# Linear attention with a token and channel mixer: kv products of two late units in one string, and weights split straight from their fp64 bits

## The chip, the cores and the metric

The kernel runs on one core of one Trainium2 chip. The metric is device time in microseconds (us) of one execution. Three runs of the kernel before gave 778.94, 780.80 and 781.54 us; their median is 780.8 us. Engines go by the profile's names: PE is TensorE (matrix products), PEld its weight loads, DVE is VectorE, ACT is ScalarE, POOL is GpSimd, and SP is SyncE, whose only work here is to issue DMAs in order.

## The reference

```
q, k, v: (8 batches, 8 heads, 576 rows, 64), float32
qs = softmax of q over the 64 columns;   ks = softmax of k over the 576 rows
kv = ks^T v     (64 x 64 for each head); attn = qs kv
x  = attn as (8, 576, 512)
h  = relu(x^T w_tok1) w_tok2;            u   = x + h^T     (w_tok1 576 x 256)
h2 = relu(u w_ch1) w_ch2;                out = u + h2      (w_ch1 512 x 1536)
```

The four weight matrices arrive as 64-bit floats and are brought to 32 bits on the chip. Products that need more than one pass of precision are made with a high part and a low part of each operand (`c1h`, `c1l` and so on), in the form fp32r.

## The kernel before

**Units.** Two heads of one batch are a unit: 32 units, four to a batch. A unit runs five stages: s1 turns q and makes kv (`stage_kv`), s2 makes y = w_tok1 q, s3 makes h1 = y kv, and s4 and s5 make the two halves of u. Units 0 to 7 are "early": they run before the channel mixer begins. Units 8 to 31 are "late": their stages are laid between the products of the channel mixer.

**The channel mixer.** 4608 columns are cut into 9 groups of 512. Groups 0 to 4 go in steps: one step is one slice f of 128 hidden rows, twelve products in `ch1` (L524) and twelve in `ch2` (L709), each 128 x 128 by 128 x 512. Groups 5 to 8 go in two pairs by a scheme with seven products in place of eight (`both_groups`, products at L753). The dictionaries `todo` and `laters` say behind which step or product each unit's stage is issued. The stages of a unit follow those of the unit before at a distance of two steps.

**kv (L377).** For each of five row blocks and each of the two heads a product of 128 x 64 weights (a slice of exp(k)) with 65 columns of v (the last one is all ones and gives the sum). Each product is plain fp32 and stands in the trace as two PE instructions, so a unit has 20. A late unit's k is loaded by `load_unit`, shifted by its maxima in `shift_k` (DVE, L338) and exponentiated (ACT, L339). The maxima come from a transposed copy of k: `find_top` reduces it and writes 128 numbers to DRAM (`line`), `spread` reads them back to all partitions (`top`, L334). `spread(n + 1)` stands in s1 of unit n. The late units share one v tile, so `load_v(n + 1)` (L215) comes behind the kv products of unit n. After the products DVE takes the reciprocal of the sums and two ACT instructions write kv into `kv_ring[0]`; `split` makes `kvh` and `kvl`.

**Weights.** `load_weights` and `load_wide` bring 512 or 1024 words of 64 bits to a raw tile, and `narrow` makes fp32 of them: the exponent (DVE L262, ACT L263), the sign (DVE L264), the mantissa (DVE L265, L267) and their product (DVE L269). `split` then copies that to the high part (ACT, L141) and subtracts to get the low part (DVE, L142). The result of `narrow` lies in a tile `cv_s` of pool `cv`, which has two buffers; the turned q of a late unit (L416) is taken from the same pool. `load_tok1` fills fp32 tiles; `load_tok2`, `load_pair` (1024 words) and `load_ch` (512 words) fill high and low parts. `load_pair` runs four times (twice among the early units, at steps 1 and 4), `load_ch` four times (steps 7, 8, 10, 11).

**Order.** The program is traced in the order written, and a planner with a model of the engines' times then fixes the order of each engine's queue. On the chip every queue is in order and waits on semaphores. A diff of a few lines can so move instructions elsewhere too.

Of the kernel before, what the change touches and what calls it, by code (L numbers as in the profile page):

```python
# [8 lines left out]
F32 = mybir.dt.float32  # L9
F32R = mybir.dt.float32r  # L10
# [5 lines left out]
P = 128  # L16
# [4 lines left out]
def attn_mixer_kernel(ctx: ExitStack, tc: tile.TileContext, q, k, kt, v, wt, out, dims):  # L21
# [21 lines left out]
    HW = CW // 2  # L43
    AHEAD = 9
    SUMS_AT = (6.5, 11.5, 16.5, 21.5, 26.5, 29.5)
    BLOCKS1, SUMS1, BLOCKS2 = (25, 27, 29, 31, 33, 35), (28.5, 32.5, 36.5, 40.5, 44.5, 48.5), (6, 11, 16, 21, 26, 29)
# [16 lines left out]

    ident = const.tile([P, P], F32R, name="ident")
    scratch = stg.tile([P, CW, 2], U32, name="stg").rearrange("p n w -> p (n w)").bitcast(F32)
    make_identity(nc, scratch[:, 0:P])
    nc.vector.tensor_copy(ident, scratch[:, 0:P])
    def v_tile(pool):
        t = pool.tile([P, C1, 2, D + 1], F32, name="v_t")
# [9 lines left out]
    ebias = const.tile([P, 1], F32, name="ebias")  # L79
    nc.gpsimd.memset(ebias, -(896.0 + 20.0) * 2.0**23)  # L80

    def kv_tile(pool, i):
# [4 lines left out]

    kv_ring = [kv_tile(const, 0)]

# [65 lines left out]

    conv = [(stg, cv)]
    first = []
# [39 lines left out]
    def load_unit(b, j):  # L197
        n = b * NJ + j
        u = {"b": b, "j": j, "n": n, "early": n < NE, "kept": {}}
        pool = early if u["early"] else ld  # L200
        if u["early"]:
            u["kt"] = load_kt(n, pool)
        u["q"] = q_of.pop(n) if n in q_of else load_q(n, pool)
        t = pool.tile([P, C1, P], F32, name="k_t")
        if not u["early"]:
            loaded[:] = [nc.sync.dma_start(t.rearrange("p c d -> p (c d)"), k[n]).ins]
        u["k"] = t
        return u

    v_of = {}  # L210

    def load_v(n):
        if n < NU and n not in v_of:
            t = v_ring[n % 2 if n < NE else 0]
            nc.sync.dma_start(t.rearrange("p c h d -> p (c h) d")[:, :, 0:D], v[n].rearrange("p c (h d) -> p (c h) d", h=2))  # L215
            v_of[n] = t
# [54 lines left out]


    N1 = C * TOK // CW
    AT_T1, AT_T2, AT_TAIL, AT_C1 = 0, N1, N1 + NT, N1 + NT + 2
# [18 lines left out]
    def load_tok2():  # L293
        if WIDE2:
            t = load_wide(AT_T2).rearrange("p (n s) -> p n s", n=NT)
            split(w2h[:, :, 0:S0], w2l[:, :, 0:S0], t, nc.vector)
        else:
            for n in range(NT):
                split(w2h[:, n, 0:S0], w2l[:, n, 0:S0], load_weights(AT_T2 + n), nc.vector)
        t = load_weights(AT_TAIL + 1, NT * TL).rearrange("p (n t) -> p n t", n=NT)  # L300
        split(w2h[:, :, S0:S], w2l[:, :, S0:S], t, nc.vector)

    def load_pair(f):
        t = load_wide(AT_C1 + f)
        (wh, wl), i = c1[f]
        split(*(w[:, i : i + 2].rearrange("p f n m -> p (f n m)") for w in (wh, wl)), t, nc.vector)
        (wh, wl), i = c2[f]
        split(*(w[:, i : i + 2].rearrange("p f m -> p (f m)") for w in (wh, wl)), load_wide(AT_C2 + f), nc.vector)
# [26 lines left out]

    def shift_k(u):
        kx = u["k"]
        nc.vector.tensor_tensor(kx, kx, top.unsqueeze(1).broadcast_to([P, C1, P]), op=ALU.subtract)  # L338
        nc.scalar.activation(kx, kx, AF.Exp)  # L339
# [30 lines left out]
    def stage_kv(u):  # L370
# [17 lines left out]
        u["kvf"] = kvf  # L388
        if u["early"]:
            return  # L390
        kvh = wk.tile([P, P], F32R, name="kvh")
# [506 lines left out]
    def begin(n):  # L898
        if n < NU and n not in units:
            units[n] = load_unit(n // NJ, n % NJ)  # L900

# [6 lines left out]
    def soft_k(n):  # L908
        if n < NU:
            with behind(drained if n > NE + 1 else []):  # L910
                shift_k(units[n])
# [27 lines left out]
    wide_pools[:] = [early_pools.enter_context(tc.tile_pool(name=n, bufs=2)) for n in ("stg_w", "cv_w")]  # L939
    conv[:] = [(stg, cv), (None, cv)]  # L940
# [3 lines left out]
    kv_ring += [kv_tile(early1, i) for i in range(1, NB)]  # L944

# [16 lines left out]
    load_tok2()  # L962
    conv[:] = [(stg, cv)]
    for n in range(NE):
# [14 lines left out]
    early_pools.close()  # L979
    del v_ring[1:], kv_ring[1:]  # L980
    ld = ctx.enter_context(tc.tile_pool(name="ld", bufs=2))
# [15 lines left out]
    def begin_first():  # L997
# [3 lines left out]
        find_top(NE)  # L1001
        find_top(NE + 1)

    def prepare():
        spread(NE, [])
        soft_k(NE)
        soft(NE)

# [5 lines left out]
    for n in range(NE, NU):  # L1014
# [8 lines left out]
        put(at[0], s1)  # L1023
        put(at[0] - 1.5, lambda n=n: find_top(n + 2))
# [21 lines left out]
    for r, (b0, b1, x0, dx) in enumerate(SPACE):  # L1046
        for i, n in enumerate(range(b0 * NJ, b1 * NJ)):
            s1, *rest = pe_stages(n)
            for x, fns in zip(
                (-2, 0, 4, 2, 4, 6, 8),  # L1050
                ((lambda n=n: find_top(n + 2),), (s1, lambda n=n: soft(n + 1)), (lambda n=n: soft_k(n + 1),), *((fn,) for fn in rest)),
            ):
                laters[r].setdefault(max(0, int(x0 + dx * i + x)), []).extend(fns)
            laters[r].setdefault(int(x0 + dx * i + 2), []).append(lambda n=n: begin(n + 2))
    for p, x in enumerate(SUMS_AT):
        if isinstance(x, float):
# [7 lines left out]
    for i, (g, f) in enumerate(steps):  # L1064
        if i in load_at:
            if load_at[i] == F_MORE:
                more_pools.close()
                c2_rows(F_MORE, NF)
                c1_rows(F_MORE, F_LAST, None)
            conv[:] = [(next_raw if load_at[i] == F_MORE + 1 else stg, cv)]  # L1070
            if load_at[i] == F_LAST:
# [90 lines left out]
```

## Time and profile before

| what | value |
|---|---|
| median of three runs | 780.8 us |
| the profiled execution | 779.16 us |
| its span, first to last instruction | 777.0 us |
| PE busy | 756.4 us (97%) |
| DVE busy | 582.4 us (75%) |
| ACT busy | 362.2 us (47%) |
| POOL busy | 39.7 us (5%) |
| chain that ended last: PE / DVE / DMA | 72% / 14% / 9% of the span |

The 2.16 us between span and time lie around the instructions. A PE product's row shows it from start to modelled end, so consecutive rows overlap: what a product costs is the distance from its start to the next one's start.

### The profile page before, as it was taken

What the parts mean: (1) busy time and instruction counts of PE and PEld (TensorE: products, weight loads), DVE (VectorE), ACT (ScalarE), POOL (GpSimd) and SP (SyncE); (2) the same over time, 40 slices, a digit from 0 to 9 for tenths busy, and PEclk for the clock granted to TensorE, in tenths of its full rate; (3) what the DMA queues carried; (4) which work ended last, traced back from release to release, by engine and by line L of the source; (5) the groups of instructions that cost most, each with busy time, mean ns of one, the idle gap of its engine ahead of it and who ended that gap; (6) DMA issues with size and microseconds to landing.
All of it is one profiled execution on the core that took longest, in us unless ns stands there. A gap on an engine that the chain in (4) does not pass through costs nothing.

```text
span 777.0 us, 12214 instructions
## 1 busy us (share of the span) xinstructions
PE 756.4 (97%) x4272; PEld 636.9 (82%) x4272; DVE 582.4 (75%) x1082; ACT 362.2 (47%) x746; POOL 39.7 (5%) x40
## 2 busy tenths in 40 slices
PE   3999999999999999999999999999999999999998
PEld 2788888888888888888888888887888888887886
DVE  7989999968899556588686697694656968447962
ACT  4677433433444433345444355445567533447510
POOL 0000000000100100001000001000000000000000
PEclk9999999999999999999999999999999999999999
DMA  9754543145768765767776689818877788768674
GB/s 299 216 166 143 186 154 102 42 123 179 240 180 275 227 191 176 209 188 208 249 253 198 177 267 302 282 44 283 244 215 236 213 242 279 222 193 295 180 228 160
DMA packets 149629, 160.61 MB, mean 207 GB/s; under 512 B 51776, under 2 KB 104128, under 8 KB 149568
## 3 DMA queue, kind: packets, MB, share of 16 engines
q1 hardware_dynamic: 140160, 146.44, 61.7%
q10 hardware_dynamic: 9408, 13.39, 4.7%
q8 instruction: 34, 0.56, 0.3%
q14 instruction: 27, 0.22, 0.1%
HBM read 116.26 MB, written 43.53 MB: 206 GB/s over the span
## 4 chain that ended last, share of the span: by engine, by line
PE 72%; DVE 14%; DMA 9%; ACT 1%; issue 1%; SPq 1%; ACTq 0%; DVEq 0%
PE b L753 28%; PE ps_h L524 12%; PE ps_o L709 12%; PE ps_h L492 7%; PE ps_h L444 4%; PE ps_h L377 2%; DMA q_t<-in_q 2%; DMA q<-cv_s 2%; PE pu L492 1%; PE ps_h L452 1%; PE ps_o L492 1%; DVE h L528 1%; DVE cv_s L264 1%; DVE st L346 1%; DMA kt_t<-in_kt 1%
## 5 line engine op out<-in xcount | busy, mean ns | idle before, releaser
L709 PE MATMUL ps_o<-h,c2h 128*128 128x512 f32 x480 | 158.9, 391 | 0.0
L753 PE MATMUL b<-uh,ring 128*128 128x512 f32 x480 | 147.9, 391 | 0.0
L709 PEld LDWEIGHTS ps_o<-h,c2h 128*128 128x128 f32 x480 | 89.8, 188 | 18.8 <-DVE stg L730 0.5
L753 PEld LDWEIGHTS b<-uh,ring 128*128 128x128 f32 x480 | 89.0, 188 | 17.9
L524 PE MATMUL ps_h<-uh,c1h 128*128 128x512 f32 x240 | 95.2, 397 | 0.1
L709 PE MATMUL ps_o<-h,c2l 128*128 128x512 f32 x240 | 93.5, 392 | 0.0
L524 PE MATMUL ps_h<-uh,c1l 128*128 128x512 f32 x240 | 93.5, 390 | 0.0
L524 PE MATMUL ps_h<-ul,c1h 128*128 128x512 f32 x240 | 93.4, 390 | 0.0
L753 PE MATMUL b<-ul,ring 128*128 128x512 f32 x240 | 92.5, 390 | 0.0
L142 POOL TENSOR_TENSOR ql<-q_t,qh 128x640 fp32r<-128x640 f32 x24 | 37.9, 1581 | 533.8 <-ACT qh L141 356.8
L528 DVE SCALAR_TENSOR_TENSOR h<-ps_h,h 128x512 fp32r<-128x512 f32 x60 | 40.9, 682 | 19.5 <-ACT h L527 19.5
L524 PEld LDWEIGHTS ps_h<-ul,c1h 128*128 128x128 f32 x240 | 45.0, 188 | 9.5
L753 PEld LDWEIGHTS b<-ul,ring 128*128 128x128 f32 x240 | 45.1, 188 | 9.5
L524 PEld LDWEIGHTS ps_h<-uh,c1h 128*128 128x128 f32 x240 | 45.1, 188 | 8.9 <-ACT c1h L141 0.5
L709 PEld LDWEIGHTS ps_o<-h,c2l 128*128 128x128 f32 x240 | 45.1, 188 | 8.9
L524 PEld LDWEIGHTS ps_h<-uh,c1l 128*128 128x128 f32 x240 | 45.2, 188 | 8.4
L527 ACT ACTIVATE h<-ps_h 128x512 fp32r<-128x512 f32 x60 | 35.5, 592 | 31.4 <-PE ps_h L524 19.8
L346 DVE TENSOR_REDUCE st<-q_t 128x10 f32<-128x640 f32 x32 | 26.0, 814 | 28.8 <-DMA q_t<-in_q 28.8
L339 ACT ACTIVATE k_t<-k_t 128x640 f32<-128x640 f32 x24 | 17.8, 740 | 41.0 <-DVE k_t L338 41.0
L753 PE MATMUL b<-c2h,ring 128*128 128x512 f32 x112 | 34.7, 391 | 0.6 <-ACT hb L746 0.4
L356 ACT ACTIVATE q_t<-q_t 128x640 f32<-128x640 f32 x32 | 23.6, 738 | 23.8 <-DVE q_t L347 21.7
L746 ACT ACTIVATE hb<-hb 128x512 f32<-128x512 f32 x36 | 22.7, 632 | 24.5 <-DVE hb L802 10.7
(268 smaller groups left out, 1546.1 us busy)
## 6 DMA issues: line engine op xcount, KB each, us to landing
ring<-w SPq DMA_DIRECT2D x84, 256.0 KB, 3.7
ring<-v SPq DMA_DIRECT2D x84, 256.0 KB, 3.5
kt_t<-in_kt SPq DMA_DIRECT2D x32, 320.0 KB, 4.5
q_t<-in_q SPq DMA_DIRECT2D x32, 320.0 KB, 3.8
v_t<-in_v SPq DMA_DIRECT2D x32, 320.0 KB, 4.8
stg_w<-in_w SPq DMA_DIRECT2D x18, 512.0 KB, 6.7
k_t<-in_k SPq DMA_DIRECT2D x24, 320.0 KB, 4.4
q<-cv_s SPq DMA_DIRECT2D x24, 320.0 KB, 3.9
```

What stands on the lines that cost most here:

```text
L142: lo_eng.tensor_tensor(lo, src, f32(hi), op=ALU.subtract)
L339: nc.scalar.activation(kx, kx, AF.Exp)
L346: nc.vector.tensor_reduce(st[:, 0, :], qt, axis=AX.X, op=ALU.max)
L356: nc.scalar.activation(qc, qc, AF.Exp)
L444: nc.tensor.matmul(y[:, 0:TOK], a, w, start=(i == 0), stop=(i == len(mm) - 1))
L492: nc.tensor.matmul(t[:, 0:N], a, w, start=(i == 0), stop=(i == len(mm) - 1))
L524: nc.tensor.matmul(t, a[:, n, :], w, start=(i == 0), stop=(i == 3 * NJ - 1))
L527: nc.scalar.activation(hh, t, AF.Relu).ins,
L528: nc.vector.scalar_tensor_tensor(hl, t, 0.0, f32(hh), op0=ALU.max, op1=ALU.subtract).ins,
L709: m = nc.tensor.matmul(o, a[:, cs], w, start=(first and i == 0), stop=(last and i == 2))
L746: nc.scalar.activation(c, c, AF.Relu)
L753: nc.tensor.matmul(outs[0 if one else n], a, b, start=first and i == 0 and (n == 0 or not one), stop=last and i == 2 and (n == 1 or not on ...
```

## The change

**kv of two late units in one string.** `stage_two` makes the products of units n and n + 1 (n even) one after the other into one PSUM bank, takes one reciprocal over both columns of sums and writes two kv tiles; `keep_kv` makes the high and low part of one unit when its s1 comes. For that the odd unit's inputs are there two steps sooner: `spread(n + 2)` stands in s1 of unit n, k is loaded by `load_k`, the late units have two v tiles (the second is a new tile `shared`), and `load_v(n + 2)` and `load_v(n + 3)` are issued one and three steps behind the even unit's s1.

**Weights.** `raw_parts` takes the place of `narrow` and `split` for all but `load_tok1`: the 64-bit word's upper half, without its last eight bits, is rebiased on ACT (L263 before) into the bits of a float, from which ACT writes the high part at once; DVE then forms what the high part leaves of the mantissa and multiplies by the power of two for the low part.

**Tiles.** Pool `cv` has one buffer; `shared` serves as the second one for conversions until the last weights are in, then as the second v tile. The identity matrix is made later in the program, in a pool that closes with the early units; `kv_ring` has two constant tiles.

```
-    cv = ctx.enter_context(tc.tile_pool(name="cv", bufs=2))
+    cv = ctx.enter_context(tc.tile_pool(name="cv", bufs=1))
+    shared = const.tile([P, C1, 2, D + 1], F32, name="shared")
...
+    def raw_parts(raw, hi, lo, s, view=lambda t: t):
+        w0, w1 = raw[:, :, 0], raw[:, :, 1]
+        nc.vector.tensor_scalar(s, w1, 0x7FFFFF00, None, op0=ALU.bitwise_and)
+        nc.scalar.activation(s, s, AF.Relu, bias=rbias, scale=8.0)
+        nc.vector.scalar_tensor_tensor(s, w1, 0x80000000, s, op0=ALU.bitwise_and, op1=ALU.bitwise_or)
+        nc.scalar.activation(hi, view(s.bitcast(F32)), AF.Copy, scale=2.0**20)
+        nc.vector.tensor_scalar(w1, w1, 0x1FF, 0x100, op0=ALU.bitwise_and, op1=ALU.bitwise_xor)
+        f1 = w1.bitcast(F32)
+        nc.vector.scalar_tensor_tensor(f1, w0, 2.0**-32, w1, op0=ALU.mult, op1=ALU.add)
+        nc.vector.tensor_scalar(s, s, 0xFF800000, None, op0=ALU.bitwise_and)
+        nc.vector.scalar_tensor_tensor(lo, view(f1), -256.0, view(s.bitcast(F32)), op0=ALU.add, op1=ALU.mult)
...
     def load_ch(f):
         h_, l_ = (w.rearrange("p n m -> p (n m)") for w in c1_row(f))
-        split(h_, l_, load_weights(AT_C1 + f), nc.vector)
-        split(*c2_row(f), load_weights(AT_C2 + f), nc.vector)
+        load_parts(AT_C1 + f, h_, l_)
+        load_parts(AT_C2 + f, *c2_row(f))
...
-        if u["n"] != NE - 1:
-            load_v(u["n"] + 2 if u["n"] < NE else u["n"] + 1)
+        if u["n"] < NE - 1:
+            load_v(u["n"] + 2)
...
+    def stage_two(*both):
+        kv = ps_unit()[:, 0 : 2 * P].rearrange("p (i x) -> p i x", i=2)
+        for i, u in enumerate(both):
+            for c in range(C1):
+                for h in range(2):
+                    hs = slice(h * D, (h + 1) * D)
+                    nc.tensor.matmul(
+                        kv[hs, i, 0 : D + 1], u["k"][:, c, hs], v_of[u["n"]][:, c, h, :], start=(c == 0), stop=(c == C)
+                    )
+        rs = sm.tile([P, 2], F32, name="rs2")
+        nc.vector.tensor_scalar(rs, kv[:, :, D], 1e-9, None, op0=ALU.add)
+        nc.vector.reciprocal(rs, rs)
+        for i, u in enumerate(both):
+            u["kvf"] = kv_ring[i]
+            for h in range(2):
+                hs = slice(h * D, (h + 1) * D)
+                nc.scalar.activation(kv_ring[i][hs, hs], kv[hs, i, 0:D], AF.Copy, scale=rs[hs, i : i + 1])
...
         def s1():
             stage_qT(units[n])
-            if n >= NE:
-                spread(n + 1, turned_in)
-            stage_kv(units[n])
+            if n < NE:
+                stage_kv(units[n])
+                return
+            spread(n + 2, turned_in)
+            if n % 2 == 0:
+                stage_two(units[n], units[n + 1])
+            keep_kv(units[n])
...
+        v_ring.append(v_tile(None))
+        load_v(NE + 1)
...
         put(at[0], lambda n=n: soft(n + 1))
-        put(at[0] + 1, lambda n=n: soft_k(n + 1))
+        put(at[0] + (SK0, SK1)[n % 2], lambda n=n: soft_k(n + 2))
         put(at[0] + 0.5, lambda n=n: begin(n + 2))
+        if n % 2 == 0:
+            put(at[0] + LK, lambda n=n: load_k(n + 3))
+            put(at[0] + LV0, lambda n=n: load_v(n + 2))
+            put(at[0] + LV1, lambda n=n: load_v(n + 3))
```

Here LK is 1.5 steps, LV0 is 1, LV1 is 3, and SK0 and SK1 are 1.5 and 0.5. In the first pair of groups the same loads are put 4 and 8 products behind the even unit's s1.

## Rows read from the trace of the kernel before

**Rows 1.** The page, part 1: busy time, share of the span, instructions.

```profile
PE 756.4 (97%) x4272; PEld 636.9 (82%) x4272; DVE 582.4 (75%) x1082; ACT 362.2 (47%) x746; POOL 39.7 (5%) x40
```

**Rows 2.** Busy time by stretch: PE, PEld, DVE, ACT, POOL, clock, DMA share, GB/s.

```profile
0.00:30.00 30.00, 15.54 (x88) 12.18 (x88) 25.60 (x58) 15.62 (x30) 1.79 (x16) 1.00 0.88 271
...
80.00:160.00 80.00, 80.00 (x361) 66.56 (x360) 74.58 (x117) 33.46 (x52) 1.56 (x1) 1.00 0.37 126
160.00:480.00 320.00, 319.35 (x2032) 273.83 (x2030) 243.46 (x484) 138.38 (x315) 30.10 (x19) 1.00 0.70 213
```

**Rows 3.** Timeline of PE, one kv string: start, us, engine, line, tiles, count.

```profile
277.33 0.61 PE L709 MATMUL ps_o<-h,c2h 128*128 128x512 f32 x2
277.79 0.39 PE L709 MATMUL ps_o<-h,c2l 128*128 128x512 f32 x1
278.10 0.80 PE L377 MATMUL ps_h<-v_t,k_t 128*64 128x65 f32 x20
278.84 0.72 PE L709 MATMUL ps_o<-h,c2h 128*128 128x512 f32 x2
279.40 0.40 PE L709 MATMUL ps_o<-h,c2l 128*128 128x512 f32 x1
```

**Rows 4.** Timeline of PE, the second piece of unit 31's kv.

```profile
590.64 0.39 PE L753 MATMUL b<-ul,ring 128*128 128x512 f32 x1
590.96 0.57 PE L377 MATMUL pu<-v_t,k_t 128*64 128x65 f32 x12
591.46 0.72 PE L753 MATMUL b<-uh,ring 128*128 128x512 f32 x2
592.02 0.40 PE L753 MATMUL b<-ul,ring 128*128 128x512 f32 x1
```

**Rows 5.** Timeline of PE, a string of plain fp32 products over the whole array.

```profile
240.07 0.39 PE L709 MATMUL ps_o<-h,c2h 128*128 128x512 f32 x1
240.30 0.60 PE L452 MATMUL ps_h<-kvf,ys 128*128 128x128 f32 x4
...
241.21 0.39 PE L524 MATMUL ps_h<-ul,c1h 128*128 128x512 f32 x1
```

**Rows 6.** Timeline of PE: the first two late units, starts that came late.

```profile
162.33 1.08 PE L709 MATMUL ps_o<-h,c2h 128*128 128x512 f32 x4
163.53 0.49 PE L524 MATMUL ps_h<-uh,c1h 128*128 128x512 f32 x1
...
177.34 0.39 PE L524 MATMUL ps_h<-ul,c1h 128*128 128x512 f32 x1
178.06 0.80 PE L377 MATMUL ps_h<-v_t,k_t 128*64 128x65 f32 x20 [0.33 <-ACT k_t L339]
```

**Rows 7.** Groups by line and shape on DVE: count, busy us, mean ns, idle before.

```profile
L267 DVE SCALAR_TENSOR_TENSOR stg_w<-stg_w 128x1024 f32<-128x1024 uint32 x8 | 9.7, 1217 | 0.0
L269 DVE TENSOR_TENSOR cv_w<-stg_w,cv_w 128x1024 f32<-128x1024 f32 x8 | 9.7, 1212 | 0.0
L269 DVE TENSOR_TENSOR cv_s<-stg,cv_s 128x512 f32<-128x512 f32 x9 | 6.2, 687 | 0.1
L265 DVE TENSOR_SCALAR stg_w<-stg_w 128x1024 uint32<-128x1024 uint32 x8 | 5.5, 684 | 0.0
L265 DVE TENSOR_SCALAR stg<-stg 128x512 uint32<-128x512 uint32 x10 | 4.2, 422 | 0.1
```

**Rows 8.** The chain that ended last, by time: start, length, what.

```profile
27.10 0.60 DVE cv_s L269
```

**Rows 9.** Timeline of DVE: the last weight conversion's last instruction.

```profile
165.63 0.65 DVE L142 TENSOR_TENSOR c2l<-cv_s,c2h 128x512 fp32r<-128x512 f32 x1
```

**Rows 10.** The loads of v, all 32.

```profile
DMA to landing us min/median/max: 3.7/4.8/8.3
```

**Rows 11.** SP's own waits: total us, times, longest us.

```profile
SPq L215 <- PE ps_h L377: 52.2, 18, 10.0
...
SPq L179 <- DMA line<-kt_t: 27.7, 10, 7.2
```

More of the change, by code (lines that the diff above doesn't have):

```diff
@@ L80, in attn_mixer_kernel @@
     nc.gpsimd.memset(ebias, -(896.0 + 20.0) * 2.0**23)
+    rbias = const.tile([P, 1], F32, name="rbias")
+    nc.gpsimd.memset(rbias, 2.0**10 - (896.0 + 20.0) * 2.0**23)
     def kv_tile(pool, i):
@@ L86, in kv_tile @@
         return t
-    kv_ring = [kv_tile(const, 0)]
+    kv_ring = [kv_tile(const, i) for i in range(2)]
     w1h = const.tile([P, C, TOK], F32R, name="w1h")
@@ L203, in load_unit, with load_k @@
         u["q"] = q_of.pop(n) if n in q_of else load_q(n, pool)
-        t = pool.tile([P, C1, P], F32, name="k_t")
-        if not u["early"]:
+        u["k"] = pool.tile([P, C1, P], F32, name="k_t") if u["early"] else k_of.pop(n)
+        return u
+    k_of = {}
+    def load_k(n):
+        if n < NU and n not in k_of and n not in units:
+            t = ld.tile([P, C1, P], F32, name="k_t")
             loaded[:] = [nc.sync.dma_start(t.rearrange("p c d -> p (c d)"), k[n]).ins]
-        u["k"] = t
-        return u
+            k_of[n] = t
     v_of = {}
@@ L270, in narrow, with load_parts, load_wide_parts @@
         return z
+    def load_parts(i, hi, lo, n=CW, view=lambda t: t):
+        if not wide:
+            split(hi, lo, view(load_weights(i, n)), nc.vector)
+            return
+        conv.append(conv.pop(0))
+        raw = raw_tile(conv[-1][0])
+        nc.sync.dma_start(raw[:, 0:n, :].rearrange("p n w -> p (n w)"), wt[i][:, 0:n].bitcast(U32))
+        s = conv[-1][1].tile([P, C1 * P], U32, name="cv_s")[:, 0:n]
+        raw_parts(raw[:, 0:n], hi, lo, s, view)
+    def load_wide_parts(i, hi, lo):
+        if not wide:
+            split(hi, lo, load_wide(i), nc.vector)
+            return
+        raw = wide_pools[0].tile([P, 2 * CW, 2], U32, name="stg_w")
+        flat = raw.rearrange("p n w -> p (n w)")
+        for x in range(2):
+            nc.sync.dma_start(flat[:, x * 2 * CW : (x + 1) * 2 * CW], wt[i + x].bitcast(U32))
+        raw_parts(raw, hi, lo, wide_pools[1].tile([P, 2 * CW], U32, name="cv_w"))
+    def raw_parts(raw, hi, lo, s, view=lambda t: t):
[9 more added lines that the diff above has]
+        nc.vector.scalar_tensor_tensor(lo, view(f1), -256.0, view(s.bitcast(F32)), op0=ALU.add, op1=ALU.mult)
     N1 = C * TOK // CW
@@ L899, in begin @@
         if n < NU and n not in units:
+            if n >= NE:
+                load_k(n)
             units[n] = load_unit(n // NJ, n % NJ)
@@ L910, in soft_k @@
             with behind(drained if n > NE + 1 else []):
[L911 removed]
+                shift_k(units[n]["k"] if n in units else k_of[n])
     def pe_stages(n):
@@ L943, in attn_mixer_kernel @@
     v_ring.append(v_tile(early1))
-    kv_ring += [kv_tile(early1, i) for i in range(1, NB)]
+    kv_ring += [kv_tile(early1, i) for i in range(2, NB)]
     stages = [pe_stages(n) for n in range(NE)]
@@ L1006, in prepare @@
         soft_k(NE)
+        spread(NE + 1, [])
+        soft_k(NE + 1)
         soft(NE)
@@ L1050, in attn_mixer_kernel @@
                 (-2, 0, 4, 2, 4, 6, 8),
-                ((lambda n=n: find_top(n + 2),), (s1, lambda n=n: soft(n + 1)), (lambda n=n: soft_k(n + 1),), *((fn,) for fn in rest)),
+                ((lambda n=n: find_top(n + 2),), (s1, lambda n=n: soft(n + 1)), (lambda n=n: soft_k(n + 2),), *((fn,) for fn in rest)),
             ):
@@ L1054, in attn_mixer_kernel @@
             laters[r].setdefault(int(x0 + dx * i + 2), []).append(lambda n=n: begin(n + 2))
+            if n % 2 == 0:
+                laters[r].setdefault(int(x0 + dx * i + 4), []).insert(0, lambda n=n: load_k(n + 3))
+                for x in (4, 8):
+                    laters[r].setdefault(int(x0 + dx * i + x), []).append(lambda n=n, x=x: load_v(n + 1 + x // 4))
     for p, x in enumerate(SUMS_AT):
```

47 lines of the change are left out of this document (25 added, 22 removed).

## The prediction

> **What bounds the kernel now.** I read the page first, then busy time by stretch, then the timeline of PE around kv. PE is busy for 97% of the span [rows 1], and by stretch it is full from 80 us on: 80.00 of 80 us, then 319.35 of 320 [rows 2]. In those stretches time goes only where PE's own queue loses it, so what counts is the distance between the starts of its products. Before 30 us it is otherwise: PE is busy for 15.54 us of 30, DVE for 25.60 [rows 2], and the chain of waits runs over DVE there, the weights' L269 with 0.60 us among its links [rows 8]. Between 80 and 160 us DVE has 74.58 of 80 us, nearly all of it weights, yet PE loses nothing to it until the very end.
>
> **A kv string.** Products of 512 columns start 0.23 us apart (277.33 to 277.79 holds two) [rows 3]. From 277.79 to 279.40, 1.61 us, PE makes three of them and the 20 instructions of kv; 1.61 - 3 x 0.23 = 0.92 us are kv's. In the piece of 12 instructions it is 592.02 - 590.64 - 0.69 = 0.69 us [rows 4]. The difference, 0.23 us for 8 instructions, is 0.029 us each; 0.92 - 20 x 0.029 = 0.34 us and 0.69 - 12 x 0.029 = 0.34 us are left. So each string pays about 0.35 us (by the unrounded starts) once, whatever its length: 0.09 before the first product, 0.05 at it, and 0.21 behind the last. The 24 late units have 28 such strings: unit 29 is in four pieces and unit 31 in two, the others are whole; one whole and one piece are shown.
>
> The Trainium skill has a rule for this (TensorEngine Tiling (Array Packing), Tiling Modes, Key Properties): to change the tiling mode drains the engine, to change only the tile within a mode does not. kv's weights are 128 x 64 tiles. Plain fp32 products over the whole array show no fixed cost: 241.21 - 240.07 = 1.14 us hold three 512-column products (two stand in the gap) and four of these, 0.45 us or 0.11 each [rows 5]. By the rule the second unit behind the first one in a string pays nothing. If a unit's start paid it instead, nothing would be saved; against that stands that the piece of 12, which only goes on with a unit begun before, pays the same 0.34 us [rows 4].
>
> **Part 1, fewer strings.** No product is added or taken away. With whole strings 24 of them become 12: 12 x 0.35 = 4.2 us off PE's queue, in stretches where PE is the bound, so off the time. The four extra pieces of before (4 x 0.35 = 1.4 us) are the planner's doing; a string of 40 may be cut as well. I take 0.7 us for them, bounds 1.4 and nothing. In all -4.9 us; the bound on the other side is a planner that cuts every pair in two: 28 strings become 24, -1.4 us.
>
> DVE loses 12 small additions and 12 reciprocals; nobody waits for these long. kv of the even unit comes later by the odd unit's ten products (20 x 0.029 = 0.58 us) and two more ACT writes. It is wanted for h1 one and a half steps on; a step is half the distance of two units, (278.10 - 178.06) / 12 = 8.3 us by the strings of two units six apart [rows 3, 6], so 12 us cover it. Cost 0.
>
> **Part 2, the odd unit's inputs sooner.** `load_k`, `load_v`, `spread` and `find_top` issue the same DMAs as before, only earlier or in another order of SP's queue; DVE and ACT do the same shifts. The leads shrink. v of the odd unit is asked for one step, 8.3 us, ahead of its string; from issue to landing it takes 4.8 us at the median, 8.3 at the longest [rows 10]. So 3.5 us are to spare at the median and none at the worst. On the other side one kind of wait goes: SP stood for 52.2 us at v's load until kv had released the one tile [rows 11]; with two tiles the load is issued behind a string that is long done. k of unit n + 2 has one step between load and shift, where it had two and a half, and its loads are as large as v's. The maxima are reduced 1.5 steps, 12 us, before `spread` sends them on, with one DMA of 512 bytes between. I take 0 for all of these in the steady part; bounds from -0.5 us (less blocking on SP) to a wait at each string, the second rival.
>
> Late starts: the string at 178.06 came 0.72 us behind the product before it where 0.32 is usual (277.79 to 278.10): 0.40 us [rows 6, 3]. That was unit 9, waiting for exp(k); in a pair its k is asked for before the first one's string. Of 0.40 I take 0.2 as saved, since the pair can as well wait for its later half; bounds 0.4 and nothing.
>
> **The first pair** is the one place with a new wait. The second v tile is also a conversion buffer, so v of unit 9 can be asked for only when the last conversion has read it. That ends at 166.28 us now [rows 9], while unit 8's string runs behind the product of 163.53 [rows 6], at 163.95. With the weights' gain (part 3) of some 3.4 us it ends near 162.9; two small memsets on POOL, the DMA and its landing of 4.8 us make about 168. If PE's queue has the string where it is now, PE waits 4 us, and up to 7.3 (166.28 + 0.2 + 4.8 - 163.95) without the weights' gain. But other products stand ready at that time, the channel mixer's steps above all, and the planner knows the chain; before, its worst miss at kv was 0.40 us. The one buffer left in `cv` is met here too: unit 9's turned q waits on DVE until the DMA has taken unit 8's, with the drains of the steps queued behind it; later units are 16 us apart and don't meet. I take +0.5 us for both, bounds 0 and 7.3.
>
> **Part 3, weights.** For each conversion DVE had two one-scalar operations, two with two tensors and a scalar, and two of two tensors (the product L269 and the subtraction in `split`). Now it has three, three and none: one L269-like instruction becomes an L265-like one, and the other keeps its price (the new last instruction is of L267's kind, 1217 ns against 1212) [rows 7]. For 1024 words that is 1212 - 684 = 0.53 us less, for 512 words 687 - 422 = 0.26 [rows 7]. Eight wide and ten narrow ones: 8 x 0.53 + 10 x 0.26 = 6.8 us of DVE. The new mask runs in place on dense words, L265 on words 8 bytes apart; the dense one may be faster (the gain up to 0.1 us more each) or, at worst, as slow as L269 (no gain). ACT keeps two instructions; the high part is ready before the mantissa is, so the trip DVE to ACT to DVE at the end is hidden behind two DVE instructions (an L265 and an L267).
>
> Where it counts: after 80 us, four wide and eight narrow ones, 4 x 0.53 + 8 x 0.26 = 4.2 us, less 0.8 for the odd unit's shift, which moves ahead: 3.4. PE waits for these weights just once, at 163.53, where four products from 162.33 should have let it go on at 163.24: -0.3 us [rows 6]. The rest is hidden by PE's own work. Before 30 us the link of 0.60 us at 27.10 [rows 8] becomes one of 0.33: -0.3 us; bounds -2.3 (the 2.6 us that DVE saves before 80 us, two narrow and four wide, all on the path, less the 0.3) and +1, if another order at the start costs. The identity is made behind a few more small memsets on POOL, which has 1.79 us of work in the first 30 us [rows 2]; its first user waits for a load of k and its exponential meanwhile. Cost 0.
>
> **The sum** against the profiled execution, 779.16 us (span 777.0 and 2.16 around it): -4.9 - 0.2 + 0.5 - 0.3 - 0.3 = -5.2, so 774.0. The median of the three runs is 780.8, 1.6 above the profiled one; the runs spread over 2.6 us. Against the median: 775.6 us.
>
> **The rivals.**
> - *The planner cuts the pairs.* For it: two units in `both_groups` are cut now. Against: 22 of 24 are whole. Each pair in two pieces gives -1.4 in place of -4.9: 780.8 - 1.7 = 779.1 us. The same side holds the case that the change saves no fixed cost (780.8 - 0.3 = 780.5), which rows 4 speak against.
> - *Slower: SP's queue ahead of the odd unit's v.* SP is in order, and a wait for `line` (L179, the next copy of k) can stand in front of this load: 27.7 us in ten waits, the longest 7.2 [rows 11]. A mean one of 2.8 fits in the 3.5 us to spare; one like the longest does not: 7.2 - 3.5 = 3.7 us at the string. If three of the 12 pairs meet such a wait, 3 x 3.7 = 11.1: 780.8 - 5.2 + 11.1 = 786.7 us. The gain is gone from 1.4 such pairs on (5.2 / 3.7), and past two of them (7.5 / 3.7) the loss is over 0.3%. For it: v's lead falls from two steps to one. Against: the 52.2 us that v's own load held the queue go, and ten such waits cost nothing now.
> - *More than the sum: the start.* If all 2.6 us that DVE saves before 80 us come off the path, and not 0.3: 775.6 - 2.3 = 773.3 us. For it: DVE is the chain before 30 us. Against: from 30 us on PE is nearly full with the early units.
>
> **How the numbers follow.** The forecast 0.60, the cut pairs 0.12 and the saving that isn't there 0.03, the slow queue 0.10, the better start 0.15. A change within 0.3% (2.3 us, about what measurements of this kernel can tell) is "same". Faster 0.60 + 0.15 = 0.75; same 0.15; slower 0.10. The range from 771.5 to 780.0 takes in the better start with the four pieces (-0.7) and most of the cut pairs, and of the first pair's wait up to 5 us; the slow queue and the unsaved cost are left out. The likeliest case alone has 773.5 to 777.7.
>
> **What would show it.** In the changed trace there should be 12 strings of 40 instructions at kv behind 160 us, each with 0.92 + 0.58 = 1.50 us of its own; PE's sum of busy time tells little, the starts do. Two of the six vector instructions of a conversion that took 1212 ns should be one of about 684 and one of 1217; the last conversion should end near 163 us, and the start at 163.53 should lose its 0.3 us. The step is wrong if strings are cut, if a second unit inside a string pays at its start, or if a string begins much more than 0.32 us behind the product before it; the prediction as a whole is wrong if PE, after 80 us, has new waits of more than 2 us in sum.

## The result and the profile after

The changed kernel takes 789.69 us (median of 6 runs, 787.96 to 792.82) beside 781.17 for the kernel before on the same chip (6 runs, 778.10 to 782.94). The ratio is 1.0125, 95% interval 1.0095 to 1.0156: slower, where 775.6 us was forecast, with a range up to 780.0. The profiled execution has a span of 786.0 us, 9.0 more than the one before.

The strings became what was forecast. The timeline of PE at the fourth string (columns: start, length, engine, line, tiles, count) shows two units in one string:

```profile
194.59 0.40 PE L586 MATMUL ps_h<-ul,c1h 128*128 128x512 f32 x1
194.92 0.80 PE L439 MATMUL ps_h<-v_t,k_t 128*64 128x65 f32 x20
195.55 0.75 PE L439 MATMUL ps_h<-shared,k_t 128*64 128x65 f32 x20
196.23 0.50 PE L771 MATMUL ps_o<-h,c2h 128*128 128x512 f32 x1
196.57 0.40 PE L771 MATMUL ps_o<-h,c2l 128*128 128x512 f32 x1
```

From 194.59 to 196.57 two 512-column products and the string take 1.98 us, so the string takes 1.52 of its own, where 1.50 was forecast; two strings of before take 2 x 0.92 [rows 3].

Yet PE is as full as before, for longer. The page's first part, and busy time by stretch (columns as in [rows 2]), the last two rows being short stretches around 245 us:

```profile
PE 762.1 (97%) x4272; PEld 638.9 (81%) x4272; DVE 572.4 (73%) x1058; ACT 361.6 (46%) x746; POOL 41.8 (5%) x43
```

```profile
160.00:480.00 320.00, 315.91 (x1999) 271.27 (x1998) 229.63 (x448) 134.82 (x306) 31.65 (x21) 0.99 0.70 211
...
244.00:249.00 5.00, 1.55 (x9) 1.11 (x7) 1.57 (x4) 0.71 (x2) 0.00 (x0) 0.88 0.96 327
249.00:254.00 5.00, 5.00 (x13) 4.14 (x14) 5.00 (x9) 2.23 (x4) 0.00 (x0) 0.50 1.03 357
```

Two things are new. **First, the products themselves start further apart.** In the late rounds (groups 5 to 8, L753 before and L815 now) PE hardly stops. The timeline of PE at 701 us, before and after:

```profile
700.88 0.61 PE L753 MATMUL b<-uh,ring 128*128 128x512 f32 x2
701.33 0.39 PE L753 MATMUL b<-ul,ring 128*128 128x512 f32 x1
701.56 0.61 PE L753 MATMUL b<-uh,ring 128*128 128x512 f32 x2
```

```profile
701.33 0.40 PE L815 MATMUL b<-ul,ring 128*128 128x512 f32 x1
701.56 0.63 PE L815 MATMUL b<-uh,ring 128*128 128x512 f32 x2
702.03 0.40 PE L815 MATMUL b<-ul,ring 128*128 128x512 f32 x1
702.26 0.63 PE L815 MATMUL b<-uh,ring 128*128 128x512 f32 x2
702.73 0.40 PE L815 MATMUL b<-ul,ring 128*128 128x512 f32 x1
```

Before, 701.56 - 700.88 = 0.68 us hold three products, 0.227 each. After, 702.73 - 701.33 = 1.40 us hold six, 0.233 each; by the unrounded starts the mean between 640 and 680 us is 234.3 ns, and 226.7 in the kernel before. The granted clock is 1.00 in both.

**Second, PE stops once for 3.5 us and then runs at half clock.** PE, then ACT, then the chain of waits (start, length, what), all of the changed kernel:

```profile
245.18 0.30 PE L554 MATMUL ps_h<-qth,kvl 128*128 128x320 f32 x1
248.94 0.79 PE L771 MATMUL ps_o<-h,c2h 128*128 128x512 f32 x1 [3.45 <-ACT h L589]
249.53 0.63 PE L771 MATMUL ps_o<-h,c2l 128*128 128x512 f32 x1
249.96 0.63 PE L771 MATMUL ps_o<-h,c2h 128*128 128x512 f32 x1
```

```profile
241.07 0.30 ACT L410 CAST qh<-ql 64x128 fp32r<-64x128 f32 x1 [0.98 <-POOL ql L147]
247.85 0.39 ACTq L794 DMA_DIRECT2D out<-part  x1
248.29 0.60 ACT L589 ACTIVATE h<-ps_h 128x512 fp32r<-128x512 f32 x1 [6.92 <-DMA w<-c1h]
```

```profile
242.04 1.33 SPq L606
243.42 4.36 DMA w<-c1h
247.85 0.39 ACTq L794
248.29 0.61 ACT h L589
```

ACT does nothing for 6.92 us: at the head of its queue stands the first output DMA of group 0 (`out_end`, L794). Its data were written by DVE at 242.27, but it leaves at 247.85, as soon as a copy of weight blocks to DRAM (`keep_blocks`, L606) has landed, though it reads nothing of that copy. Behind it in ACT's queue waits the drain of `h` (the copy out of PSUM, L589) that PE needs. In the kernel before SP issues that copy behind the output (timelines of ACT and of SP):

```profile
239.83 0.40 ACTq L732 DMA_DIRECT2D out<-part  x1
```

```profile
251.64 0.49 SPq L544 DMA_DIRECT2D w<-c1h  x1
```

When PE starts again it has stood for 3.45 us, the granted clock is 0.50, that is 1.2 GHz, and 512-column products start 0.43 us apart (249.53, 249.96). From 248.94 to 254.99 it makes twelve of them and four of 320 columns; at full clock these take 12 x 0.227 + 4 x 0.147 = 3.31 us, here 6.05, so 2.7 are lost beside the stop.

To see what each part is worth I added up, in the traces, the distances between the starts of PE's products behind 80 us: 512-column products against 226.7 ns each, the strings' own time, and what all other long distances have over their usual one. In us:

```
                       before   after   e5    e16
512-column products      1.7    12.0    2.3    2.1
strings                 24.6    19.1   19.0   19.0
stops, half clock        4.5     9.5    8.8    7.4
last product starts    773.2   782.1  772.4  771.6
```

(e5 and e16 are experiments below.) After against before: +10.3 - 5.5 + 5.0 = +9.8, beside 9.0 of span.

### The profile page after: what moved, and what is told of

Same layout as the page of the kernel before. It is cut to its first block, busy times and chain, and to the rows that moved or that the text cites. A ratio compares the mean times of both kernels' runs of the same rounds, so it can differ in the third digit from the quotient of the medians.

```text
span 786.0 us, 12206 instructions
## 1 busy us (share of the span) xinstructions
PE 762.1 (97%) x4272; PEld 638.9 (81%) x4272; DVE 572.4 (73%) x1058; ACT 361.6 (46%) x746; POOL 41.8 (5%) x43
## 4 chain that ended last, share of the span: by engine, by line
PE 84%; DVE 6%; DMA 4%; ACT 2%; issue 1%; SPq 1%; ACTq 0%; DVEq 0%
PE b L815 29%; PE ps_o L771 19%; PE ps_h L586 19%; PE ps_h L554 6%; PE ps_h L506 4%; DMA q_t<-in_q 2%; PE ps_h L439 1%; PE pu L554 1%; PE ps_h L514 1%; DMA stg_w<-in_w 1%; PE ps_o L554 1%; DMA top<-line 1%; PE pu L506 1%; PE ps_o L506 1%; DMA w<-c1h 1%
## 5 line engine op out<-in xcount | busy, mean ns | idle before, releaser
L771 PE MATMUL ps_o<-h,c2h 128*128 128x512 f32 x480 | 161.9, 396 | 3.5 <-ACT h L589 3.5
L815 PE MATMUL b<-uh,ring 128*128 128x512 f32 x480 | 150.4, 397 | 0.6 <-ACT hb L862 0.6
L771 PEld LDWEIGHTS ps_o<-h,c2h 128*128 128x128 f32 x480 | 91.1, 190 | 23.5 <-ACT h L589 3.7
L815 PEld LDWEIGHTS b<-uh,ring 128*128 128x128 f32 x480 | 89.3, 188 | 21.4 <-ACT hb L862 0.8
L586 PE MATMUL ps_h<-uh,c1h 128*128 128x512 f32 x240 | 96.5, 403 | 0.6 <-ACT kvf L449 0.6
L771 PE MATMUL ps_o<-h,c2l 128*128 128x512 f32 x240 | 94.8, 395 | 0.0
L586 PE MATMUL ps_h<-ul,c1h 128*128 128x512 f32 x240 | 94.6, 394 | 0.0
L586 PE MATMUL ps_h<-uh,c1l 128*128 128x512 f32 x240 | 94.5, 394 | 0.0
L815 PE MATMUL b<-ul,ring 128*128 128x512 f32 x240 | 93.6, 396 | 0.0
L147 POOL TENSOR_TENSOR ql<-q_t,qh 128x640 fp32r<-128x640 f32 x24 | 39.7, 1652 | 476.5 <-ACT qh L146 385.8
L589 ACT ACTIVATE h<-ps_h 128x512 fp32r<-128x512 f32 x60 | 35.7, 595 | 50.2 <-PE ps_h L586 38.5
L815 PEld LDWEIGHTS b<-ul,ring 128*128 128x128 f32 x240 | 45.2, 188 | 10.9
L586 PEld LDWEIGHTS ps_h<-ul,c1h 128*128 128x128 f32 x240 | 45.2, 188 | 10.4
L771 PEld LDWEIGHTS ps_o<-h,c2l 128*128 128x128 f32 x240 | 45.6, 190 | 9.0
L586 PEld LDWEIGHTS ps_h<-uh,c1h 128*128 128x128 f32 x240 | 45.2, 188 | 9.5 <-ACT kvf L449 0.8
L586 PEld LDWEIGHTS ps_h<-uh,c1l 128*128 128x128 f32 x240 | 45.3, 189 | 8.7
L815 PE MATMUL b<-c2h,ring 128*128 128x512 f32 x112 | 35.1, 396 | 0.0
```

The costliest lines, as they stand in the source:

```text
L147: lo_eng.tensor_tensor(lo, src, f32(hi), op=ALU.subtract)
L586: nc.tensor.matmul(t, a[:, n, :], w, start=(i == 0), stop=(i == 3 * NJ - 1))
L589: nc.scalar.activation(hh, t, AF.Relu).ins,
L771: m = nc.tensor.matmul(o, a[:, cs], w, start=(first and i == 0), stop=(last and i == 2))
L815: nc.tensor.matmul(outs[0 if one else n], a, b, start=first and i == 0 and (n == 0 or not one), stop=last and i == 2 and (n == 1 or not on ...
```

## The experiments

All ratios are to the kernel before on the same chip, with 95% intervals. The names e1 to e16 are the labels' beginnings. First, the addresses. The changed constants (`shared`, `rbias`, `rs2`, one `cv` buffer less) move every tile at the left end of SBUF by 160 bytes; the right end stays, where c1 of the first eight slices lies and later `ring`, the tiles from which the late rounds take their weights. What the programs give as addresses:

```
                 uh0 (left)   ring0, c1h0 (right)   moved against each other, bytes
before             46464           196480                  0
after              46624           196480                160
```

**e1, e2, e3: is it an alignment?** Both kernels have pad tiles; these are the edits, `shift` at the left end, `edge` at the right.

```
e1 (after):   -const.tile([P, 96], F32, name="shift")   +const.tile([P, 104], F32, name="shift")
e2 (before):  the same edit
e3 (before):  the same edit, and "edge" from [P, 24] to [P, 32]
```

> The changed kernel with one unused constant tile 32 bytes longer: every tile allocated from the left end of SBUF then starts at a multiple of 64 bytes again, as before the change; the order of every queue is the same as in the changed kernel. Theory A (the 512-column products slowed from 227 to 229-234 ns because left-hand tiles came to start 32 bytes off a multiple of 64): the products at the last matmul line go back to 227 ns, 1007 of them times 7.3 ns and 720 of the first channel product times 4.5 ns, about 10 to 11 us less than the changed kernel, 778 to 780 us. Theory B (the slower spacing comes from the clock or from what else reads memory at that time, not from addresses): no change, 789 us.

> The kernel before with the same tile 32 bytes longer: its left-hand tiles, which start at multiples of 64 bytes, are moved 32 bytes off; nothing else differs. Theory A: its 512-column products with weights from the right end (first channel product, slices 0 to 7, and all products of the pairs) go from 227 to about 234 ns, 10 to 11 us more, 791 to 792 us. Theory B: no change, 781 us.

> The kernel before with tiles of both ends moved 32 bytes off a multiple of 64. If what counts is the distance of the weights' address from the moving operand's (each mod 64), products stay at 227 ns: 781 us. If what counts is that the moving operand alone starts at a multiple of 64, they go to 234 ns everywhere, the second channel product too: 794 us or more. If it is the weights' start alone, the kernel of the run with only the left end moved is not slowed and this one is.

Measured: e1 787.68 us, 1.0101 (1.0087 to 1.0114), where theory A had 778 to 780; e2 787.83, 1.0100 (1.0084 to 1.0115); e3 781.79, 1.0036 (1.0023 to 1.0049). So 32 bytes in the kernel before, with nothing else changed, cost 8.7 us, and moving both ends gives most of it back; but e1, at a multiple of 64, is as slow. A simple alignment isn't it.

**e7, e8: the distance between the ends.** The same pad of the kernel before, 64 and 128 bytes larger.

```
e7: "shift" [P, 96] -> [P, 112]      e8: "shift" [P, 96] -> [P, 128]
```

> The kernel before with its pad 'shift' 64 bytes larger; nothing else changes. Left-end tiles then lie 64 bytes (of 256) past the right-end ones, as when both ends were moved by 32 bytes apart, but the right end stands on a multiple of 128. Theory (the distance counts, not where either stands): 229 ns per pairs-stage product, 781 to 782.5 us, ratio 1.003 to 1.004. Rival (each operand's own alignment counts): 233 ns and 787 to 788 us, as with 32 bytes at the left end alone.

> The kernel before with its pad 'shift' 128 bytes larger. Theory (distance, with a period of 128 bytes): 227 ns, 779 us, no change. If the period is 256 bytes: anything between the 229 ns of 64 bytes and the 233 ns of 192, so 782 to 788 us. Rival (each operand's own alignment to 128 bytes counts): 227 ns, 779 us.

Measured: e7 781.77, 1.0033 (1.0019 to 1.0048); e8 785.42, 1.0077 (1.0059 to 1.0096). e3 and e7 have the same distance at different places and the same time: at these 64 bytes the distance between left and right end decides, not where either stands. A period of 128 bytes, by which e8 would be at 779 us, is out; whether 256 bytes would be as good as none, no run tests. Mean start to start of a late-round product, 640 to 680 us, by the bytes that the left end has moved against the right one:

```
moved       0      32     64        128    160    192
kernel    before   e2   e3, e7      e8    after   e1
ns        226.7  233.3  228.9,228.9 232.3  234.3  233.3
```

Products whose operands both lie at the left end are spared: the second mixer product (L771, `h` and c2) has a median of 227 ns in the changed kernel too. The first one (L586) takes `uh` from the left end and c1 from the right for slices 0 to 7, from the left for slices 8 to 11: in the changed kernel the first eight have means of 233.4 to 234.0 ns, the last four 227.2 to 228.6; before, all have 227.1 to 228.4.

**e5: the change at the old addresses.**

```
-    const.tile([P, 96], F32, name="shift")
+    const.tile([P, 56], F32, name="shift")
```

> The changed kernel with its pad 'shift' 160 bytes smaller, so that every tile that lives at the left end of SBUF has the address that it has in the kernel before; the order on each queue is that of the changed kernel. Theory (distance between weights and columns): the 512-column products that take one operand from the left end and one from the right (ffn products of the pairs stage and six of eight chunks of the first product of the early rounds) go back from 233 to 234 ns to 227 ns, some 9 us less than the changed kernel: 778 to 779.5 us beside 779.2 us of the kernel before. The stop of the PE at 245 us and the half clock behind it stay, since ScalarE's queue still waits there. Rival (the order of work slows the products): 787.5 to 788 us, spacing as in the changed kernel.

Measured: 779.99 us, 1.0004 (0.9991 to 1.0017). The order of the instructions on every queue is that of the changed kernel; with 160 bytes the measured loss is gone. The timeline of PE, as above:

```profile
700.82 0.62 PE L815 MATMUL b<-uh,ring 128*128 128x512 f32 x2
701.27 0.39 PE L815 MATMUL b<-ul,ring 128*128 128x512 f32 x1
701.50 0.62 PE L815 MATMUL b<-uh,ring 128*128 128x512 f32 x2
```

Again 0.68 us hold three products. The stop near 245 us stays (2.6 us, clock of the span 0.997), and the 5 us of the strings don't show.

**e4, e6, e9: the output elsewhere.** Group 0's four output DMAs leave ACT's queue: for SP's at the addresses of e1 (e4) and of e5 (e6), for GpSimd's at those of e5 (e9).

```
-            nc.scalar.dma_start(out[g, n], t)
+            (nc.sync if g == 0 else nc.scalar).dma_start(out[g, n], t)      # e9: nc.gpsimd
```

> The changed kernel with the 64-byte start and with the four output DMAs of group 0 issued from SP in place of ACT. Theory C (the 3.5 us stop of PE near 245 us, and the half clock behind it, come from ACT standing 6.9 us in front of such a DMA, which waits for an unrelated DMA of the same semaphore): the stop and the half clock go, some 6 us less than the run with the 64-byte start alone, 772 to 774 us. If PE's stop has another cause (the inputs of the pair), it stays: 778 to 780 us.

> The same, and the four output DMAs of group 0 issued by SP instead of ScalarE. Theory of two causes: both are gone, and the saving of the shorter string order shows alone: 227 ns spacing, no stop of more than 1 us at 245 us, granted clock 1.0; 774 to 776.5 us, ratio 0.994 to 0.997. Rival (the strings save nothing): 779 us, no difference from the kernel before.

> The changed kernel with its left-end tiles back at the addresses of the kernel before, and the four output DMAs of group 0 issued by GpSimd, whose queue holds nothing then that the PE waits for, instead of ScalarE. Theory (the strings save what was forecast, and SP's late loads ate it when the output went to SP): no PE stop over 1 us near 245 us, clock 1.0, PE waits behind 80 us some 2 to 3 us in sum as in the kernel before and not the 7 us of the run with SP; 773.5 to 775.5 us beside 779.5, ratio 0.992 to 0.995. Rival (the new order of work brings its own waits wherever the output goes): 778 to 779.5 us.

Measured: e4 785.55, 1.0074 (1.0059 to 1.0088), 2.1 us less than e1, where 6 were expected; e6 778.93, 0.9993 (0.9980 to 1.0006); e9 777.64, 0.9975 (0.9962 to 0.9988). The stop of over 2 us near 245 us is gone in all three, and the half clock behind it too; but e6 and e9 win 0.6 and 1.3 us, not 5. (The planner answered these edits with another order: at 137 of its 4272 places PE's queue holds another instruction than in the changed kernel.) PE's waits behind 80 us in e9 (total us, times, longest; the kernel before has 1.6 us of waits there in all):

```profile
PE ps_h L586 <- ACT kvf L449: 2.5, 3, 1.0
PE b L815 <- ACT hb L862: 1.3, 1, 1.3
PE b L815 <- DMA ring<-v: 1.1, 1, 1.1
PE ps_o L771 <- DVE h L590: 0.8, 1, 0.8
```

The first kind is the joined string's bank: it comes free only when its four copies to `kvf` (L449) are done. In e6 it is 3.0 us.

**e10, e11, e12, e13: the two parts alone.** e10 is e9 with the conversion of before; e11 is e9 with one string per late unit; e13 is e11 with the output on ACT again; e12 is the kernel before with e9's edit, as a control.

```
e10:  -        if not wide:          (in load_parts, load_wide_parts)     +        if True:
e11:  -            if n % 2 == 0:    -                stage_two(units[n], units[n + 1])
      +            stage_two(units[n])       (with v and k of unit n + 2 asked for one at a time)
```

> The same kernel with the weights converted as in the kernel before (a full value made by six instructions, then split by two), at unchanged addresses: the joined strings alone. Theory (VectorE's shorter conversion is hidden): as with it, 773.5 to 775.5 us, within 0.3%. Rival (the conversion shortens waits of the PE on VectorE): 1 to 3 us slower than with it.

> The same kernel with the shorter conversion and one string of 20 products per late unit instead of one of 40 per two, k and v loaded one unit at a time; addresses unchanged. Theory (14 strings more at 0.35 us each): 4.9 us slower than with joined strings, 778.5 to 780 us, no difference from the kernel before. Rival (joined strings save nothing): the same time as with them.

> The kernel before with group 0's four output DMAs issued by GpSimd instead of ScalarE, as a control for the runs that have this. Theory (ScalarE does not stand at these DMAs in the kernel before, so nothing is won): 779 us, ratio 0.998 to 1.002. Rival (the gain of the run with the shorter conversion and single strings comes from here): 776 to 777 us, ratio 0.996.

> The shorter conversion with one string per late unit and two v tiles, addresses as in the kernel before, the output of group 0 back on ScalarE. Theory (the gain of 2.6 us is the conversion's, that of the shorter work of VectorE at the start and of a v tile that is free sooner): 776 to 777.5 us, ratio 0.996 to 0.998. Rival (the gain was GpSimd's queue): 778.5 to 780 us.

Measured: e10 784.82, 1.0075 (1.0055 to 1.0096); e11 776.37, 0.9965 (0.9948 to 0.9982); e12 778.85, 0.9997 (0.9980 to 1.0014); e13 778.38, 0.9991 (0.9972 to 1.0009). e11 is the fastest kernel here and beats the one before. Its theory, that without joining the strings it would be 4.9 us slower than e9, missed; the rival came true: joining the strings, with the sooner loads and the order that come with it, saves no time that these runs can see. e11's strings do take 22.8 us of PE, 3.8 more than joined ones, but PE waits less (behind 80 us, columns as above):

```profile
PE ps_o L772 <- DVE h L591: 1.1, 1, 1.1
PE b L816 <- DMA ring<-v: 0.2, 1, 0.2
```

That is 1.3 us, beside 5.7 in e9. e10 missed both expectations, and its trace says why; ACT's timeline:

```profile
181.08 4.41 ACTq L794 DMA_DIRECT2D out<-stg  x4
185.59 1.28 ACT L449 ACTIVATE kvf<-ps_h,rs 64x64 f32<-64x64 f32 x4 [5.18 <-DMA out<-stg]
```

and PE's next product waits 5.02 us for `kvf`: another order of the queues, and ACT stands at the outputs of group 1 instead. What the conversion is worth beside joined strings is therefore not shown. e12 shows no gain from GpSimd's queue alone; e11 against e13 leaves open whether the shorter conversion with the second v tile wins 0.1% or 0.35%, as their intervals meet. e13's strings take 22.8 us like e11's, and PE's long distances sum to 3.7 us in e11 and 7.1 in e13. The profiled executions took 776.06 us (e11), 781.93 (e13, median 778.38) and 781.79 (e9, median 777.64), so of the waits in e9 and e13 a part may belong to that execution alone; that e11 is not slower than e9 rests on the medians.

**e14, e16: does ACT stand for the copy?** Both are e5 with the second `keep_blocks` planned at another step.

```
-    BLOCKS1, SUMS1, BLOCKS2 = (25, 27, 29, 31, 33, 35), ...
+    BLOCKS1, SUMS1, BLOCKS2 = (25, 26, 29, 31, 33, 35), ...      # e16: (25, 28, 29, ...)
```

> The changed kernel at the addresses of the kernel before, output on ScalarE, and the one copy of weight blocks to DRAM that ScalarE's output DMA stands behind (the second, at 242 us) planned one step sooner; the order of the products is the same. Theory (ScalarE stands at the output DMA because it shares a completion counter with this copy): the copy has landed some 8 us sooner, ScalarE does not stand, no PE stop of 3 us at 244 us and no half clock behind it: 774 to 775.5 us, ratio 0.993 to 0.996. Rival (ScalarE stands for the output's own data from VectorE): the stop stays, 779 to 780 us.

> The changed kernel at the addresses of the kernel before, output on ScalarE, and the second copy of weight blocks to DRAM planned one step later, so that SP issues it behind group 0's output and the output's completion counters were last used by short loads. Theory (ScalarE stood behind that copy's counter): the output goes when its data are written, the PE stop of 3 to 4 us near 244 us and the half clock behind it are gone; the late bank releases of the joined strings stay: 776.5 to 778.5 us, ratio 0.996 to 0.999. If the forecast's 5 us for the strings are to be had whole: 774 to 775 us. Rival (the stop comes from the output's own data or from the joined string's drain): the stop stays, 779 to 780 us.

e14: 779.62, 1.0005 (0.9988 to 1.0023). SP issues the copy at 241.11 and the output leaves at 246.67 (e5: 241.30 and 245.78): the edit moved the copy by almost nothing, so it tells nothing. In e16 SP issues it behind the outputs: 778.44, 0.9992 (0.9975 to 1.0008), clock 1.00. ACT's timeline, and PE's:

```profile
239.92 0.30 ACT L410 CAST qh<-ql 64x128 fp32r<-64x128 f32 x1 [0.97 <-POOL ql L147]
244.95 0.33 ACTq L794 DMA_DIRECT2D out<-part  x1
245.33 0.60 ACT L589 ACTIVATE h<-ps_h 128x512 fp32r<-128x512 f32 x1 [5.11 <-DMA q_t<-in_q]
```

```profile
245.98 0.50 PE L771 MATMUL ps_o<-h,c2h 128*128 128x512 f32 x1 [1.43 <-ACT h L589]
```

The built programs list what the first output's DMA waits for: DVE's data, and the counter of finished DMAs that it is going to use itself. There are eight such counters for the DMAs of SP and ACT together, and the last one to use this one before it is the block copy in the changed kernel and e5, and a load of q in e16. The trace names the same two: <-DMA w<-c1h, and now <-DMA q_t<-in_q. So the cause is shown: ACT stood for another queue's DMA with the same counter. In e16 it still does, for 5.11 us and not 6.92, and the output does not go when its data are written, as was expected: 1.4 us of PE are lost, and no half clock follows.

**e15: the maxima sooner.** e9 with `find_top` of odd units one step sooner.

```
-        put(at[0] - TOP, lambda n=n: find_top(n + 2))
+        put(at[0] - (TOP, 2.5)[n % 2], lambda n=n: find_top(n + 2))
```

> The changed kernel at the addresses of the kernel before, output of group 0 on GpSimd, and for every odd unit the maxima of the keys one step sooner, so that their reduction on VectorE and their DMA on ScalarE no longer stand in front of the joined string's reciprocals and copies. Theory (the joined string's bank comes free late because its drain is queued behind the maxima, some 2.5 us in three waits): these waits go, 774.5 to 776 us, ratio 0.994 to 0.996. Rival (the waits only move): 777 to 778 us, as without it.

Measured: 777.40, 0.9984 (0.9962 to 1.0005). PE's waits for `kvf` fall from 2.5 us (e9) to 1.0, but those for the drain of `hb` (1.2) and for `ring` (1.3 in two) stay as in e9, two small ones of 0.8 in sum are new, and that for `h` falls from 0.8 to 0.2: 4.5 us in all, beside 5.7. The time is that of e9 within the intervals, not the 774.5 to 776 of the theory: what the shorter waits are worth, two medians of 777.40 and 777.64 can't tell.

What these waits are, in e16. DVE, ACT and PE around the string of 358 us:

```profile
364.13 1.23 DVE L616 TENSOR_TENSOR stg<-c1h,c1l 128x1024 f32<-128x1024 f32 x1 [2.36 <-DMA w<-stg]
365.49 0.10 DVE L444 RECIPROCAL rs<-rs 128x2 f32<-128x2 f32 x1
```

```profile
366.10 1.29 ACT L449 ACTIVATE kvf<-ps_h,rs 64x64 f32<-64x64 f32 x4 [6.59 <-DVE rs L444]
```

```profile
367.44 0.50 PE L586 MATMUL ps_h<-uh,c1h 128*128 128x512 f32 x1 [0.73 <-ACT kvf L449]
```

The reciprocal stands on DVE behind a sum of weights (L616) that waits 2.36 us until a DMA has read its buffer; the four copies, 1.29 us for two units, come 6.5 us after the string and hold the bank. And the chain of waits near 533 us:

```profile
523.01 5.85 DMA top<-line
528.88 1.09 DVE k_t L381
530.00 0.74 ACT k_t L382
...
532.83 0.50 ACT hb L862
...
533.37 1.66 PE b L815 x6
```

Here exp(k), moved sooner, waits at the head of ACT's queue for its maxima, and the drain that PE wants (L862, a copy out of PSUM to `hb`) is the fifth instruction behind it: 1.3 us.

## Why the prediction was wrong

**Right: the string.** One fixed cost per string and none at the second unit: in all 14 strings behind 160 us (11 whole ones and three pieces) the first product comes 0.32 to 0.33 us behind the product before it, forecast 0.32, and from the first to the last of 40 it is 1.16 us, of 20 0.58. The Trainium skill's rule (TensorEngine Tiling (Array Packing), Tiling Modes, Key Properties), that only a change of mode drains the engine, agrees: 20 more instructions of that mode cost 0.58 us (1.16 against 0.58) and no more. The strings take 5.5 us less, by the forecast 4.9 and 0.2. The planner cut only the first pair, in three; the rival of cut pairs fell.

**Right: the small terms.** No string begins late; unit 9's 0.40 us went, and the first pair found other products to run: no wait at 161.24, 164.70 or 170.28, where +0.5 was put. The last conversion ends at 162.83 (forecast 162.9), and the product that waited at 163.53 follows its predecessor now:

```profile
162.14 0.69 DVE L317 SCALAR_TENSOR_TENSOR c2l<-stg,shared 128x512 fp32r<-128x512 f32 x1
```

```profile
160.70 0.39 PE L771 MATMUL ps_o<-h,c2h 128*128 128x512 f32 x1
160.92 0.39 PE L586 MATMUL ps_h<-uh,c1h 128*128 128x512 f32 x1
```

Of the two instructions of 1212 ns one became a mask and the other the last instruction, 688 and 1215 ns where 684 and 1217 were said; the dense mask was no faster than that. The groups of DVE:

```profile
L316 DVE TENSOR_SCALAR cv_w<-cv_w 128x1024 uint32<-128x1024 uint32 x8 | 5.5, 688 | 0.0
L317 DVE SCALAR_TENSOR_TENSOR c1l<-stg_w,cv_w 128x1024 fp32r<-128x1024 f32 x4 | 4.9, 1215 | 0.0
```

**Wrong: "Products of 512 columns start 0.23 us apart".** The sum took this distance as a constant of the kernel. With some 2350 such distances behind 80 us, 4.4 ns more each are 10.3 us, twice what the strings save. The cause is no instruction of the change but the bytes that its new tiles add ahead of all others: e2 makes the loss without the change, e5 takes it away from the change. The prediction followed every instruction and no address; the pads `shift`, `shift_back` and `edge`, which stand in the part of the kernel that the change grows, were the hint. No rival held this. In its place the runs showed 231.9 ns on average behind 80 us, where the kernel before has 227.5, and e5 at the old addresses 227.7.

**Wrong: part 2, "I take 0 for all of these in the steady part".** It bounded the cost by waits at the strings and found none there, rightly. The waits came at three other places: the first output stands on ACT behind a block copy that SP now issues ahead of it (251.64 us in the kernel before, 242.04 after), 3.6 us and 2.7 of half clock; the joined string's bank comes free late (0.6 us here, up to 3.0 in e6); exp(k) stands in front of a drain (0.6 us here, 1.3 in e16). The prediction's own test, new waits of more than 2 us behind 80 us, came out against it: 4.7 us, where the kernel before has 1.6, and the half clock. The slow rival (786.7 us) was near the time by accident; its mechanism, the odd unit's v behind SP's queue, is in no row.

**Wrong: part 1, "off PE's queue, in stretches where PE is the bound, so off the time".** The first half held and the second did not: e9 has 3.8 us less of strings than e11 and is not faster (777.64 and 776.37 us). A full PE was not proof that what it is spared comes off the time, since the joined strings came with waits of their own: e9 has 2.5 us of them for the bank and 1.3 for the drain to `hb`, e11 none of either.

With addresses and the copy mended (e16) the account is +0.4 for products, -5.6 strings, +2.9 waits, -2.3 in all, and the span is 1.6 us shorter; the measured ratio, 0.9992 (0.9975 to 1.0008), can't tell that from nothing. So of the forecast 5.2 us more than half is eaten by new waits even then.

Open: what delays a product when the distance is off, and why 64 bytes cost least and 32 much, isn't shown. Of the late waits, only the one at the output was tied to its cause by a change made to it; the other two are read from rows. What part of the waits is the joining's and what the planner's new order, no run separates.

## What to carry to other kernels

When a change adds or resizes a tile, compare the addresses of the operands of the main products before any count of instructions: some bytes of padding can cost or return more than the change (here 1% of the time). Here a DMA issued from a compute engine's queue held that engine for another queue's DMA with the same completion counter, so see what the outputs' counters were last used by, or issue them from a queue that nobody waits for. On a full engine a saving was worth only what the next waits left: add up starts, strings and stops separately, since the median alone showed none of the three.

## What the hardware showed

- The pitch of a 512-column product at full clock depends on how its two operands lie to each other in SBUF: 226.7 ns at the addresses of the kernel before, 228.9 with 64 bytes more between them, 232.3 with 128, 233.3 with 32 or 192, 234.3 with 160.
- The program has eight completion counters for the DMAs of SP and ACT. An output DMA on ACT waited 5.6 us after its data were written (242.27 to 247.85) for an unrelated copy with the same counter.
- After PE had stood for 3.45 us the granted clock was 0.50, in all of the 5 us from 249 on (products 0.43 us apart); in e5 it was 0.50 after a stop of 2.65 us too. After the 1.43 us of e16 it stayed at 1.00.
